# A fused attention and mixture kernel on one core: the rows of the first mixture's output transposed by VectorE in 32x32 blocks and stored in 128-byte runs

## The chip, the cores and the metric

One core of a Trainium2 chip runs the whole program in one launch. The metric is the time of one execution on the device in microseconds. The engines of the core are TensorE (PE in the profile, its weight loads PEld), VectorE (DVE), ScalarE (ACT), GpSimd (POOL) and SyncE (SP), which issues all DMA transfers of this kernel.

## What is computed

Three stages, all in float32, on 2304 tokens of 512 numbers (4 batches of 576 tokens).

```python
# landmark attention, 4 batches x 8 heads x 576 tokens x 64
q_lm, k_lm = means over 18 tokens of q, k          # 32 landmarks
A, Bm, C = sm(q, k_lm), sm(q_lm, k_lm), sm(q_lm, k)
Z = six steps of Z = 2 Z - Z Bm Z                   # inverse of Bm
x = A Z C v                                         # tokens x 512
# first mixture ("moe"): a gated layer over all tokens
xn = x / rms(x) * g
x = (silu(xn @ w_gate) * (xn @ w_val)) @ w_out      # 512 -> 1536 -> 512
# second mixture ("moe2"): a token with x @ w_skip > 0 goes to its best of 8 experts
out = x;  out[t] += prob * relu(x[t] @ w1[e]) @ w2[e]
```

The output of the first mixture is needed twice: with its 512 numbers along the partitions, as the matmuls of the second mixture take it, and as rows of tokens in `out`, to which the second mixture adds.

## The kernel before

The tokens go through the first mixture in 8 units of 288 (half a batch each; `NH` = 288). For a unit, `run_unit` makes 12 blocks of the hidden layer. A block is a gate product `pg` and a value product `pv`, each of 6 matmuls into a tile of 128x288 in PSUM (four such buffers, `acc`); ScalarE takes the tanh of `pg` (`h<-pg`), VectorE does two multiplications (`h<-h,pg`, `h<-h,pv`), ScalarE and GpSimd split the result into a high and a low part (`h_t`). Then `project` makes the unit's output `o` from the 12 blocks, and `evacuate` puts it into `x2T`: 128 partitions x 4 chunks x 288 tokens, so the 512 numbers lie along partitions and chunks. There is one `x2T` buffer.

`finish(u, x2T)`, a generator that is run in pieces beside the next unit's blocks, does the rest: it stores `x2T` into the scratch tensor `xT_d` (L897), makes the logits of the second mixture (`lp`, copied to `lps`, then `lg`), and writes the tokens' rows to `out`. For each of the unit's two tiles of 128 tokens it does four 128x128 transposes on TensorE (`x2t`, L933), a copy from PSUM by VectorE (L937) and a store of 256 KB in runs of 2 KB (L938). For the last 32 tokens VectorE transposes 32x32 blocks (L924), and four stores of 16 KB in runs of 128 bytes put the blocks in place (L929). `lps` and the row buffers `x2` share one buffer. Every second unit then does the routing (`rM`, stored to `m_d`).

Beside the units run the attention of the next batch (loads `kq` and `vt`, products `sk`, `sq`, `cT`) and the products `P` of its result with the weights (loads `wl`, `wr`). In the last unit (7) the second mixture is made ready: `list_pairs` makes the list of pairs of expert and batch that have tokens (`lst`, later `rest`), SP reads it, then come the loads of the first pair's tokens (`x2r`, L1068) and first weights (`w1r`, L1048; four buffers for both), which ScalarE (`xsh<-x2r`, `P<-w1r`), GpSimd and VectorE split into high and low parts. After unit 7, `mixture` runs the first pair: products `ph` into relu, `w2r` loads of the second weights (L1061), the loads `old` of the rows of `out` (L1085), the products `py`, the stores. In this run there are three pairs, the third in a loop.

`slot` decides how far the side generators go, by running sums of estimated work on each engine (`busy`, in which a TensorE transpose counts too). A scheduler then sets the order of the instructions on each engine from the dependencies; each engine and SP's queue run their instructions strictly in that order. All instructions of the four compute engines go through one helper, so that they have one line in the profile (L59); they are told apart by their tiles' names. The profile shortens `x2` to `x`.

Of the kernel before, what the change touches and what calls it, by code (L numbers as in the profile page):

```python
# [6 lines left out]
F32 = mybir.dt.float32  # L7
# [12 lines left out]
KC, FC = DM // 128, DF // 128  # L20
E, DF2 = 8, 1024
FC2 = DF2 // 128
NH = S // 2
NQ = 3
PC = 256
UT = (128, 128, 32)
# [37 lines left out]
def attention_moe_kernel(  # L64
# [4 lines left out]
    V, A, G, PE = (  # L69
        Paced(e, busy, n)  # L70
        for e, n in (
            (nc.vector, "V"), (nc.scalar, "A"), (nc.gpsimd, "G"), (nc.tensor, "P")
        )
    )
    SP = nc.sync
# [10 lines left out]
    def b3(ap, n):  # L86
        return ap.unsqueeze(2).to_broadcast([ap.shape[0], ap.shape[1], n])
# [55 lines left out]
    def bank(name):  # L143
        return pb.tile([128, 512], F32, name=name, tag="b")
# [5 lines left out]
    ident = const.tile([128, 128], F32, name="ident")  # L150
# [583 lines left out]
    def x2_tile(dt):  # L734
        return wk.tile([128, 2, DM], dt, name="x2", tag="x2")
# [157 lines left out]
    def finish(u, x2T):  # L893

        b, half = u // 2, u % 2
        u0 = NH * u
        SP.dma_start(xT_d[:, :, u0 : u0 + NH], x2T)  # L897
        yield

        lp = bank("lp")[:, 0:NH]  # L900
        for c in range(KC):
            PE.matmul(
                lp[32 * c : 32 * c + 32, :], wcat[:, c], x2T[:, c],
                start=True, stop=True,
            )
        lps = x2_tile(F32)[:, 0, 0:NH]
        A.copy(lps, lp)
        yield
        lg = bank("lg")
        for t, m in enumerate(UT):  # L910
            PE.matmul(
                lg[0:m, 32 * t : 32 * t + E + 1], lps[:, 128 * t : 128 * t + m],
                ident4[:, 0 : E + 1], start=True, stop=True,
            )
        lg = lg[:, 0:96].rearrange("p (t e) -> p t e", t=3)[:, :, 0 : E + 1]
        A.copy(lgs[:, 3 * half : 3 * half + 2, :], lg[:, 0:2])
        A.copy(lgs[0:32, 3 * half + 2, :], lg[0:32, 2])
        yield
        for t, m in enumerate(UT):
            ts = slice(128 * t, 128 * t + m)  # L920
            if t == 2:

                x2 = x2_tile(F32)[:, 0, 0:128].rearrange("p (c d) -> p c d", c=KC)
                V.transpose(x2, x2T[:, :, ts])  # L924
                ov = out[u0 + 256 : u0 + NH, :].rearrange(
                    "t (c q d) -> q t c d", c=KC, q=4
                )
                for q in range(4):
                    SP.dma_start(ov[q], x2[32 * q : 32 * q + 32])  # L929
                continue  # L930
            pt = bank("x2t")
            for c in range(KC):
                PE.transpose(pt[0:m, 128 * c : 128 * c + 128], x2T[:, c, ts], ident)  # L933
            if t % 2 == 0:
                x2s = x2_tile(F32)
            x2 = x2s[:, t % 2]
            V.tensor_copy(x2[0:m], pt[0:m])  # L937
            SP.dma_start(out[u0 + 128 * t : u0 + 128 * t + m, :], x2[0:m])  # L938
            yield
        if half == 0:  # L940
            return

        L8 = lgs[:, :, 0:E]
        mx = rt.tile([128, NT], F32, name="rmx")
        V.tensor_reduce(mx, L8, AX.X, ALU.max)
        d = rt.tile([128, NT, E], F32, name="rd")
        V.tensor_tensor(d, L8, b3(mx, E), ALU.subtract)
        ex = rt.tile([128, NT, E], F32, name="rex")
        A.activation(ex, d, AF.Exp)
        V.scalar_tensor_tensor(d, d, 0.0, rank, ALU.is_equal, ALU.mult)  # L950
        V.tensor_reduce(mx, d, AX.X, ALU.max)
        M = rt.tile([128, NT, E], F32, name="rM")
        V.tensor_tensor(M, rank, b3(mx, E), ALU.is_equal)
        yield
        s = rt.tile([128, NT], F32, name="rs")
        V.tensor_reduce(s, ex, AX.X, ALU.add)
        V.tensor_scalar(s, s, 1e-9, None, ALU.add)
        V.reciprocal(s, s)
        V.scalar_tensor_tensor(s, lgs[:, :, E], 0.0, s, ALU.is_gt, ALU.mult)
        V.tensor_tensor(M, M, b3(s, E), ALU.mult)  # L960

        V.tensor_reduce(Ms[:, b], M.rearrange("p t e -> p e t"), AX.X, ALU.add)
        for i in range(2):
            r0 = b * S + NH * i
            SP.dma_start(
                m_d[r0 : r0 + 256, :].rearrange("(t p) e -> p t e", p=128),
                M[:, 3 * i : 3 * i + 2],
            )
            SP.dma_start(m_d[r0 + 256 : r0 + NH, :], M[0:32, 3 * i + 2])
        yield  # L970
# [230 lines left out]
    def run_unit(u, before):  # L1201
# [23 lines left out]
        for c in range(KC):  # L1225
            if u == 0:
                ps = pss[c]
            else:
                ps = accbank("o")[:, 0:NH]
                for f in range(0, FC, 2):  # L1230
                    project(c, ps, (f, f + 1))
                    slot()
            evacuate(x2T, c, ps)
        fin.append(finish(u, x2T))
        side.insert(0, fin[0])

# [178 lines left out]
```

## Time and profile before

| | us |
|---|---|
| median of 3 executions | 700.03 (697.22 to 702.12) |
| the profiled execution | 697.77 |
| its span, first to last instruction | 695.9 |
| TensorE busy in it | 644.3 (93%) |
| VectorE busy | 447.8 (64%) |
| ScalarE busy | 273.8 (39%) |
| GpSimd busy | 144.0 (21%) |
| mean granted TensorE clock | 0.960 of full speed |

Matmuls overlap, so that the busy share of TensorE is not its use at peak; a matmul of 288 columns takes 300 ns from start to end, while the next one starts some 0.13 us behind it. The granted clock is a share of the full 2.4 GHz; 0.5 is the lower level of 1.2 GHz. 1.9 us of the profiled execution lie outside the span.

### The profile page before, as it was taken

The numbers are of one execution on the slowest core, as the hardware profiler recorded it, in microseconds if no ns is written. First come the engines' busy times: TensorE is split into PE (matmuls) and PEld (weight loads), VectorE is DVE, ScalarE is ACT, GpSimd is POOL, SyncE is SP. The second block draws the span as 40 slices with busy tenths as digits, with TensorE's granted clock in tenths as the row PEclk, the third lists the DMA queues.
The fourth block names the chain that finished last, engine by engine and source line by source line (L and its number), as shares of the span: only waits on it lengthen the run. The fifth ranks groups of instructions, "written<-read, shape, count | busy, mean of one in ns | idle before, by whom it ended". The sixth has DMA issues, their size and how long they took to land.

```text
span 695.9 us, 13178 instructions
## 1 busy us (share of the span) xinstructions
PE 644.3 (93%) x4895; PEld 560.5 (81%) x4895; DVE 447.8 (64%) x1004; ACT 273.8 (39%) x613; POOL 144.0 (21%) x162
## 2 busy tenths in 40 slices
PE   4578499999999999999999999999889999999997
PEld 4456167977977988978988968899889988988985
DVE  5874999979778687895768775541623455353451
ACT  0743778433235413433422442331533253243240
POOL 4000026313201301400310211130642024022020
PEclk9755799999999999999999999999999999999999
DMA  8677574652267523176512143400541375454454
GB/s 294 230 253 244 217 247 163 179 157 73 63 154 176 145 82 116 56 174 168 127 47 67 42 108 74 128 5 35 161 124 65 103 225 186 137 155 156 138 157 154
DMA packets 79440, 97.18 MB, mean 140 GB/s; under 512 B 16016, under 2 KB 58000, under 8 KB 79376
## 3 DMA queue, kind: packets, MB, share of 16 engines
q1 hardware_dynamic: 79376, 96.33, 46.0%
q8 instruction: 39, 0.64, 0.4%
q14 instruction: 25, 0.20, 0.1%
HBM read 76.97 MB, written 19.34 MB: 138 GB/s over the span
## 4 chain that ended last, share of the span: by engine, by line
PE 75%; DVE 11%; DMA 4%; ACT 4%; issue 2%; SPq 1%; POOL 1%; DVEq 0%; ACTq 0%; POOLq 0%
PE o L59 18%; PE py L59 11%; PE ph L59 11%; PE pv L59 10%; PE pg L59 9%; PE P L59 3%; PE sq L59 2%; PE sk L59 2%; DVE wo L59 2%; PE nr L59 1%; DMA kq<-in_q_dram 1%; DVE h L59 1%; DVE rbs L59 1%; DVE P L59 1%; DMA wr<-in_moe_w_val_dram 1%
## 5 line engine op out<-in xcount | busy, mean ns | idle before, releaser
L59 PE MATMUL o<-h_t,wo 128*128 128x288 f32 x1152 | 166.1, 300 | 2.6 <-DVE h L59 1.0
L59 PEld LDWEIGHTS o<-h_t,wo 128*128 128x128 f32 x1152 | 156.7, 189 | 10.3 <-issue 5.9
L59 POOL TENSOR_TENSOR h_t<-h,h_t 128x288 fp32r<-128x288 f32 x96 | 81.8, 855 | 354.5 <-ACT h_t L59 347.3
L59 PE MATMUL pg<-ap_t,P 128*128 128x288 f32 x576 | 101.6, 305 | 14.6 <-ACT P L59 8.9
L59 PEld LDWEIGHTS pg<-ap_t,P 128*128 128x128 f32 x576 | 83.5, 191 | 26.4 <-issue 16.5
L59 PE MATMUL pv<-ap_t,P 128*128 128x288 f32 x576 | 101.1, 304 | 0.3 <-DVE h L59 0.2
L59 PEld LDWEIGHTS pv<-ap_t,P 128*128 128x128 f32 x576 | 83.7, 191 | 5.1 <-issue 3.4
L59 PE MATMUL ph<-xsh,P 128*128 128x288 f32 x384 | 78.1, 297 | 0.0
L59 DVE SCALAR_TENSOR_TENSOR h<-h,pg 128x288 f32<-128x288 f32 x96 | 42.7, 447 | 36.8 <-ACT h L59 36.3
L59 PEld LDWEIGHTS ph<-xsh,P 128*128 128x128 f32 x384 | 62.0, 188 | 0.6 <-issue 0.5
L59 ACT ACTIVATE h<-pg 128x288 f32<-128x288 f32 x96 | 39.2, 409 | 48.4 <-PE pg L59 47.1
L59 PE MATMUL ph<-xsl,P 128*128 128x288 f32 x192 | 56.8, 296 | 0.0
L59 ACT CAST h_t<-h 128x288 fp32r<-128x288 f32 x96 | 41.2, 431 | 28.4 <-DVE h L59 28.4
L59 PE MATMUL py<-wo,h_t 128*128 128x512 f32 x210 | 51.6, 396 | 0.0
L59 PEld LDWEIGHTS py<-wo,h_t 128*128 128x128 f32 x210 | 39.6, 188 | 9.7
L59 DVE TENSOR_TENSOR h<-h,pv 128x288 f32<-128x288 f32 x96 | 42.4, 448 | 6.9 <-PE pv L59 3.2
L59 DVE STREAM_TRANSPOSE T<-kq 64x576 f32<-64x576 f32 (+1 forms) x40 | 35.5, 888 | 5.9 <-DMA kq<-in_k_dram 4.4
L59 PEld LDWEIGHTS ph<-xsl,P 128*128 128x128 f32 x192 | 36.2, 189 | 0.1
L59 ACT CAST P<-P 128x512 fp32r<-128x512 f32 x48 | 26.3, 585 | 22.9 <-PE P L59 21.3
L59 POOL TENSOR_TENSOR P<-w1r,P 128x512 fp32r<-128x512 f32 x16 | 20.6, 1289 | 70.1 <-ACT P L59 70.1
L59 DVE TENSOR_TENSOR P<-P,P 128x512 fp32r<-128x512 f32 x48 | 31.6, 678 | 3.7 <-ACT P L59 3.7
L59 DVE SCALAR_TENSOR_TENSOR h_t<-ph,h_t 128x288 fp32r<-128x288 f32 (+2 forms) x45 | 14.6, 352 | 28.1 <-ACT h_t L59 28.1
(223 smaller groups left out, 903.9 us busy)
## 6 DMA issues: line engine op xcount, KB each, us to landing
wl<-wg_d SPq DMA_DIRECT2D x36, 256.0 KB, 4.7
wr<-wv_d SPq DMA_DIRECT2D x32, 256.0 KB, 5.5
w1r<-in_moe_w_dram SPq DMA_DIRECT2D x32, 256.0 KB, 3.4
wr<-in_moe_w_gate_dram SPq DMA_DIRECT2D x6, 1024.0 KB, 7.8
wr<-in_moe_w_val_dram SPq DMA_DIRECT2D x6, 1024.0 KB, 5.8
wo<-in_moe_w_dram SPq DMA_DIRECT2D x24, 256.0 KB, 5.3
kq<-in_k_dram SPq DMA_DIRECT2D x8, 576.0 KB, 4.5
kq<-in_q_dram SPq DMA_DIRECT2D x8, 576.0 KB, 3.9
```

The costliest lines, as they stand in the source:

```text
L59: return f(*args, **kw)
```

## The change

The rows of a unit are no longer made in three tiles. VectorE transposes 32x32 blocks of two chunks at a time over all 288 tokens (128 x 576 numbers to an instruction), twice for a unit. Behind each of the two come 8 stores, one for each chunk and each of its four groups of 32 partitions: 32 partitions x 9 blocks x 32 numbers, so 288 runs of 128 bytes, 36 KB. TensorE's transposes, their PSUM tile and VectorE's copies out of it are gone. The second transpose writes the single `x2` buffer that the first 8 stores read. A unit has 16 stores where there were 6, the program 128 where there were 48.

```diff
@@ finish(u, x2T) @@
-        for t, m in enumerate(UT):
-            ts = slice(128 * t, 128 * t + m)
-            if t == 2:
-                x2 = x2_tile(F32)[:, 0, 0:128].rearrange("p (c d) -> p c d", c=KC)
-                V.transpose(x2, x2T[:, :, ts])
-                ov = out[u0 + 256 : u0 + NH, :].rearrange(
-                    "t (c q d) -> q t c d", c=KC, q=4
-                )
+        ov = out[u0 : u0 + NH, :].rearrange(
+            "(a t) (c q d) -> q c t a d", t=32, c=KC, q=4
+        )
+        for c in range(0, KC, 2):
+            x2 = x2_tile(F32).rearrange("p c n -> p (c n)")[:, 0 : 2 * NH].rearrange(
+                "p (c n) -> p c n", n=NH
+            )
+            V.transpose(
+                x2.rearrange("p c n -> p (c n)"),
+                x2T[:, c : c + 2].rearrange("p c n -> p (c n)"),
+            )
+            for i in range(2):
                 for q in range(4):
-                    SP.dma_start(ov[q], x2[32 * q : 32 * q + 32])
-                continue
-            pt = bank("x2t")
-            for c in range(KC):
-                PE.transpose(pt[0:m, 128 * c : 128 * c + 128], x2T[:, c, ts], ident)
-            if t % 2 == 0:
-                x2s = x2_tile(F32)
-            x2 = x2s[:, t % 2]
-            V.tensor_copy(x2[0:m], pt[0:m])
-            SP.dma_start(out[u0 + 128 * t : u0 + 128 * t + m, :], x2[0:m])
+                    SP.dma_start(
+                        ov[q, c + i],
+                        x2[32 * q : 32 * q + 32, i].rearrange(
+                            "t (a d) -> t a d", d=32
+                        ),
+                    )
             yield
```

The scheduler's orders differ in many places, since other instructions stand between the same neighbours. Three places matter below. The lines behind L938 have moved up by one.

The first is ScalarE in unit 7, from the fourth block of the hidden layer on (`h<-pg` is the tanh of a block, `xsh<-x2r` splits a load of the first pair's tokens). Before:

```order
L59 ACTIVATE h<-pg 128x288
L59 CAST xsh<-x2r 128x576 x2
L59 CAST h_t<-h 128x288
L59 CAST xsh<-x2r 128x576
L59 ACTIVATE h<-pg 128x288
L59 CAST xsh<-x2r 128x576
L59 ACTIVATE h<-pg 128x288
```

Now, from the third block on:

```order
L59 ACTIVATE h<-pg 128x288 x2
L59 CAST h_t<-h 128x288 x2
L59 ACTIVATE h<-pg 128x288 x2
L59 CAST xsh<-x2r 128x576
L59 CAST h_t<-h 128x288
L59 CAST xsh<-x2r 128x576
L59 CAST h_t<-h 128x288
L59 CAST xsh<-x2r 128x576
L59 ACTIVATE h<-pg 128x288
L59 CAST xsh<-x2r 128x576
```

The first split stood behind four tanh of the unit and stands behind six now.

The second is ScalarE at the end of the same unit, where it splits the last four weight loads of the first pair (`P_666<-w1r`). Before:

```order
L59 CAST P_666<-w1r 128x512 x2
L59 ACTIVATE h<-pg 128x288
L59 CAST P_666<-w1r 128x512
L59 ACTIVATE h<-pg 128x288
L59 CAST P_666<-w1r 128x512
L59 CAST h_t<-h 128x288 x2
L59 ACTIVATE h<-pg 128x288
```

Now:

```order
L59 CAST P_662<-w1r 128x512 x2
L59 ACTIVATE h<-pg 128x288
L59 CAST h_t<-h 128x288
L59 CAST P_666<-w1r 128x512 x2
L59 ACTIVATE x2T<-o 128x288
L59 CAST P_666<-w1r 128x512 x2
```

The four splits stood between the unit's last three tanh and stand behind the last one now.

The third is SP's queue in the first pair of the second mixture, ahead of the last two loads of second weights (`w2r`, which begin behind the last row of the first fence and of the second fence's loads `old`). Before:

```order
L929 DMA out_dram<-x_6322 128x1x32 x4
L1085 ISA
L1085 DMA old_6480<-out_dram 128x512
L1085 ISA
L1085 DMA old_6482<-out_dram 128x512
L1085 ISA
L1085 DMA old_6484<-out_dram 128x512
L1085 ISA
L1085 DMA old_6486<-out_dram 64x512
L1061 ISA
L1061 DMA w2r<-in_moe_w_dram 128x512
```

Now:

```order
L968 DMA m_d<-rM 32x8
L1017 TENSOR_LOAD rest
L1017 ISA x2
L932 DMA out_dram<-x_6310 32x9x32 x8
L1075 ISA
L1075 DMA mc<-m_d 128x4x1
L1078 ISA
L1078 DMA mc<-m_d 64x1
L1084 ISA
L1084 DMA old_6470<-out_dram 128x512
```

A read of the list `rest` and the unit's last 8 stores now stand ahead of the loads `mc`, all five `old` and the two `w2r`.

## Rows read from the trace of the kernel before

**Rows 1.** The page: busy time by engine, and the chain by engine.

```profile
PE 644.3 (93%) x4895; PEld 560.5 (81%) x4895; DVE 447.8 (64%) x1004; ACT 273.8 (39%) x613; POOL 144.0 (21%) x162
...
PE 75%; DVE 11%; DMA 4%; ACT 4%; issue 2%; SPq 1%; POOL 1%; DVEq 0%; ACTq 0%; POOLq 0%
```

**Rows 2.** Windows of 50 us: length, busy by engine, PEclk, DMA share, GB/s.

```profile
50.00:100.00 50.00, 37.10 (x182) 23.41 (x182) 38.02 (x57) 31.00 (x54) 2.89 (x4) 0.73 0.66 230
...
250.00:300.00 50.00, 49.97 (x448) 44.03 (x442) 43.26 (x112) 16.30 (x49) 11.05 (x13) 1.00 0.26 84
...
600.00:650.00 50.00, 50.00 (x293) 44.86 (x293) 21.71 (x41) 17.84 (x35) 10.74 (x8) 1.00 0.43 135
```

**Rows 3.** TensorE in order of time: start us, us; two groups of transposes, what follows.

```profile
488.10 1.04 PE L59 MATMUL x2t<-ident,x2T 128*128 128x128 f32 x8
488.89 0.65 PE L59 MATMUL pg<-ap_t,P 128*128 128x288 f32 x3
...
543.58 0.60 PE L59 MATMUL x2t<-ident,x2T 128*128 128x128 f32 x4
...
543.94 0.38 PE L59 MATMUL ph<-xsh,P 128*128 128x288 f32 x1
...
544.16 0.29 PE L59 MATMUL ph<-xsl,P 128*128 128x288 f32 x1
```

**Rows 4.** VectorE's groups with shapes kept apart, and the small transpose by its tile.

```profile
L59 DVE COPY x<-x2t 128x512 f32<-128x512 f32 x16 | 10.6, 683 | 1.9 <-ACT h L59 1.4 <-PE x2t L59 0.4
...
L59 DVE STREAM_TRANSPOSE AT<-sT 128x576 f32<-128x576 f32 x8 | 6.2, 773 | 1.1 <-POOL sT L59 1.1
...
L59 DVE STREAM_TRANSPOSE x<-x2T x8: 293/304/311, 209.1 to 548.9; 128x128 f32<-128x128 f32 x8
```

**Rows 5.** SP's issues by line: ns min/median/max; under the first its landing.

```profile
L929 SPq DMA_DIRECT2D out_dram<-x x32: 590/600/662, 209.4 to 551.2; - x32
...
DMA to landing us min/median/max: 1.8/1.9/3.4
...
L938 SPq DMA_DIRECT2D out_dram<-x x16: 338/362/952, 163.5 to 546.0; - x16
...
L897 SPq DMA_DIRECT2D xT_d<-x2T x8: 582/594/604, 141.5 to 532.7; - x8
```

**Rows 6.** Window in which the four L929 stores of one unit are issued.

```profile
209.40:212.10 2.70, 2.70 (x23) 2.70 (x22) 2.70 (x7) 0.48 (x2) 0.00 (x0) 1.00 0.09 15
```

**Rows 7.** TensorE in unit 7, in order of time: blocks and two gaps.

```profile
490.18 0.96 PE L59 MATMUL pg<-ap_t,P 128*128 128x288 f32 x6
...
491.77 0.95 PE L59 MATMUL pg<-ap_t,P 128*128 128x288 f32 x6
...
497.31 1.81 PE L59 MATMUL pg<-ap_t,P 128*128 128x288 f32 x6 [2.22 <-DVE h L59]
...
509.69 1.07 PE L59 MATMUL pg<-ap_t,P 128*128 128x288 f32 x6 [2.70 <-DVE h L59]
```

**Rows 8.** ScalarE in unit 7, in order of time.

```profile
492.06 1.37 ACT L59 CAST xsh<-x2r 128x576 fp32r<-128x576 f32 x2 [0.19 <-DMA x2r<-xT_d]
...
495.79 0.67 ACT L59 CAST xsh<-x2r 128x576 fp32r<-128x576 f32 x1 [2.03 <-DMA x2r<-xT_d]
496.36 0.40 ACT L59 ACTIVATE h<-pg 128x288 f32<-128x288 f32 x1
...
507.73 0.62 ACT L59 CAST P<-w1r 128x512 fp32r<-128x512 f32 x1 [0.75 <-DMA w1r<-in_moe_w_dram]
508.25 0.40 ACT L59 ACTIVATE h<-pg 128x288 f32<-128x288 f32 x1
```

**Rows 9.** Windows of 5 us in unit 7; PEclk is the eighth number.

```profile
495.00:500.00 5.00, 2.78 (x12) 2.69 (x12) 2.56 (x6) 3.07 (x7) 2.72 (x3) 0.72 0.75 245
500.00:505.00 5.00, 5.00 (x38) 5.00 (x37) 3.57 (x8) 3.06 (x8) 4.54 (x4) 0.94 0.43 106
...
510.00:515.00 5.00, 5.00 (x28) 5.00 (x27) 2.24 (x5) 1.94 (x5) 3.10 (x4) 0.66 0.64 204
```

**Rows 10.** SP's issues in order of time: unit 7, then the first pair.

```profile
489.23 2.01 SPq L1068 DMA_DIRECT2D x2r<-xT_d  x4
...
554.90 0.94 SPq L1061 DMA_DIRECT2D w2r<-in_moe_w_dram  x2
```

**Rows 11.** The first pair: ScalarE's split of that load, TensorE's first use.

```profile
558.97 0.62 ACT L59 CAST wo<-w2r 128x512 fp32r<-128x512 f32 x1 [1.75 <-DMA w2r<-in_moe_w_dram]
...
561.39 1.56 PE L59 MATMUL py<-wo,P 128*128 128x512 f32 x6
```

## The prediction

> **What bounds the kernel now.** I read the page first: TensorE is busy 93% of the span, and the chain that ends last is 75% TensorE and 11% VectorE [rows 1]. The windows of 50 us say where: up to about 100 us it waits for others and gets a lower clock (0.73 in the second window), but from 250 to 300 us and from 600 to 650 us it has no idle time [rows 2]. The transposes that go lie between 153 and 544 us, all in that part. There, time taken off TensorE's queue comes off the run, unless the new work makes TensorE wait. So the next views were TensorE in order of time, for what a transpose costs and for gaps, then ScalarE and SP around the gaps.
>
> **TensorE's transposes.** 64 of them go, in 12 places: 8 groups of four and 4 of eight. A group of eight holds the queue from 488.10 to 488.89 us, 0.79 us, a group of four from 543.58 to 543.94, 0.36 us [rows 3]. 4 x 0.79 + 8 x 0.36 = 6.0 us. The first matmul behind such a group takes 0.38 us where its neighbour takes 0.29 [rows 3]; twelve times 0.09 are 1.1 us more, part of which another switch of shape would cost anyway. Other groups last somewhat longer than the two shown. Bounds 6.0 to 7.4, taken: **-6.8 us**.
>
> **VectorE.** Out: 16 copies of 0.683 and 8 small transposes of 0.304 us, together 13.4 us. In: 16 transposes of 128 x 576; the same operation and shape from SBUF to SBUF takes 0.773 us [rows 4], together 12.4 us. VectorE has slack in the stretches where TensorE is full, so -1.0 us of busy time is worth nothing: **0**. Per 128x128 block TensorE is the cheaper engine, 0.36 / 4 = 0.09 us of its queue against 0.773 / 4.5 = 0.17 us [rows 3, 4]. The Trainium skill ("VectorE: DVE Perf Modes", Rules for kernel authors) says to use TensorE for a 128x128 transpose where the result may go to PSUM, which speaks against this change. By its rule the work would be left where it is, and the sum would be 0; the rows agree with it on the price of a block alone, but TensorE's result has to be copied out by VectorE, and TensorE is the full engine.
>
> **SP's queue.** Out for a unit: 2 stores of 0.362 and 4 of 0.600 us, 3.1 us. In: 16 stores of 288 runs. No row shows that shape. The nearest is L929, also 32 partitions in runs of 128 bytes, 0.600 us with 128 runs; the store of `x2T` has 512 runs and takes 0.594 us [rows 5], so the time does not grow with the runs. I take 0.60, bounds 0.36 (as L938) and 1.35 (0.60 x 288 / 128, if it did grow). At 0.60 a unit's stores take 9.6 us, 6.5 us more than before, 52 us in the program. SP mostly waits for others, so only what stands behind the stores matters (below). Moving the bytes is cheap: while the four L929 stores go out, the 16 DMA engines are busy 0.09 of 2.7 us, 3.9 engine-us, at 15 GB/s, 40 KB or 316 runs [rows 6]: 12.3 ns a run. A unit's 4608 runs are 3.5 us of all engines, spread over 9.6 us of issue. The Trainium skill ("DMA: Bandwidth & Descriptors", Issuing engines are not separate DMA queues) calls the time to start a DMA usually small beside the DMA itself. Here a row says otherwise, 0.60 us to issue against 18 runs x 12.3 ns = 0.22 us on each engine; by the page the delays priced next would be near 0 and the time 1.8 us lower.
>
> **The added wait.** The second transpose of a unit waits on VectorE until the first 8 stores have landed: 8 x 0.60 + 1.9 = 6.7 us [rows 5] behind the first. Behind it in VectorE's queue stand the multiplications of the blocks, for which TensorE's PSUM buffers wait. In the new order the fewest blocks between the two are about five (units 1 and 3), at 1.59 us each, from 490.18 to 491.77 [rows 7], 8.0 us; in units 5 and 7 they make up 9.6 us, in the others some 20 to 40 instructions stand between. So the wait is covered, by 1.2 us at the least: **0**. The cover is gone from 0.76 us an issue on.
>
> **Unit 7.** Here TensorE stands still twice for multiplications on VectorE, 2.22 and 2.70 us [rows 7]. VectorE waits for the tanh on ScalarE, and that stands behind splits of loads: 2.03 us for `x2r`, then the tanh at 496.36; later `w1r`, then the tanh at 508.25 [rows 8]. After each gap the clock falls to the lower level for a while: mean 0.72, 0.94 and 0.66 in three windows of 5 us [rows 9], 1.4 + 0.3 + 1.7 = 3.4 us. Both together cost 8.3 us. In the new order the first split stands two tanh later, 3.2 us, and the last four `w1r` splits stand behind the last tanh. Against that, `x2r` itself comes later: the list's instructions on VectorE stand behind the 0.773 us transpose and a further block's multiplications, so I put the loads of 489.23 [rows 10] at some 490.5 to 491. The third load then lands about 1.2 to 1.7 us later than before, at 497, while its tanh would be due at some 495.5; TensorE has two blocks of PSUM in hand and stands still for about 0.8 us. The second gap goes, since what its splits wait for is no longer ahead of a tanh. Left are 0.8 us and perhaps one fall of the clock, 1.7: gain 5.8 to 7.5. Bounds +2 (the loads later still) and -8.3; since the landing is guessed, I take **-5.0 us**.
>
> **First pair.** The last two `w2r` now come behind the list `rest`, 8 stores and all of `old`. `rest` is read near 550 in the old clock, then 8 x 0.60, two `mc` and five `old` at some 0.5 us each: 560.8 in place of 554.90 [rows 10]. The old load was split 4.1 us after its issue [rows 11]; now that is 564.9, and 1.9 us more for the two parts give 566.8. TensorE begins `py` at 561.39 [rows 11] and in the new order does 30 matmuls that need no part of them first, 6.4 us at 0.21 us, and all this 0.8 us earlier: needed at about 567. Bounds 0 to +3, taken **+0.7**. Loads of `kq`, `vt`, `wl` and `wr` that stand behind stores in the other units come 2 to 6 us later; most are fetched long ahead: 0 to +3, taken **+1.1**.
>
> **Sum:** -6.8 - 5.0 + 0.7 + 1.1 = -10.0 us on the profiled 697.77. That execution is 2.3 us under the median; I take the same off the median of 700.03: **690.0 us**.
>
> **Rivals.**
> *Unit 7 keeps its gaps.* Loads later by as much as the splits have been moved leave both gaps: -6.8 + 1.8 = -5.0, 695.0. For it: ScalarE's order follows the scheduler's idea of when loads land, and the trace shows it 2.03 us too early before. Against it: the second gap's splits have left their place altogether.
> *More goes.* All 8.3 us of unit 7 and the delays at 0: -15.1, 684.9.
> *The loads come much later in unit 7*, the gaps grow by 3 us and the clock falls once more: -6.8 + 1.8 + 4.7, 699.7.
> *SP becomes the bound (slower).* If issue grows with the runs, 1.35 us, the wait of the second transpose is 8 x 1.35 + 1.9 = 12.7 us. In units 1 and 3 VectorE stops for 4.7 us, in 5 and 7 for 3.1; less 1.6 us of matmuls in hand that is 3.1, 3.1, 1.5 and 1.5 us of TensorE, and four falls of the clock at 1.7: 16.0 us. `w2r` comes 8 x 0.75 = 6 us later still and TensorE waits for it: +6.7 in place of 0.7. 16.0 + 6.7 - 6.8 = +15.9, 715.9. It decides from 0.76 us an issue on. Against it: 0.594 us for 512 runs [rows 5].
>
> **How the numbers follow.** Forecast 0.45; gaps kept 0.30; more 0.13; loads much later 0.06; SP the bound 0.06. About 1% (7 us) is what a measurement of this kernel can tell from no change, so faster by over 1% is below 693.0. That holds for nearly all of the forecast, for more, and for a fifth of the first rival, whose price is uncertain by some 3 us: 0.41 + 0.13 + 0.06 = 0.60. Slower by over 1% is the last rival alone, 0.06; within 1% the rest, 0.34. The range of 684.5 to 697.5 takes in the forecast, the first rival and most of "more".
>
> **What would show it.** No `x2t` on TensorE; issue of the new stores at 0.60 us; VectorE's idle time ahead of the second transposes under 1 us in all; the two gaps at `pg` in unit 7 under 2 us together, and a clock near 1.00 there; `py` of the first pair starting on `w2r` in time. I am wrong if the new stores take over 0.76 us to issue, if ScalarE still waits for `x2r` ahead of a tanh, or if the new orders open gaps where there were none.

## The result and the profile after

The new kernel takes 688.74 us (median of 4 runs, 686.14 to 691.38) against 699.82 for the old one beside it: a ratio of 0.985, 95% interval 0.982 to 0.9881. A second series gave 0.9898, 0.9874 to 0.9923. So it is about 7 to 11 us faster; 690.0 had been forecast.

The page of the new kernel, engines and chain, answers to [rows 1]:

```profile
PE 638.6 (93%) x4831; PEld 552.4 (80%) x4831; DVE 452.9 (66%) x996; ACT 275.1 (40%) x613; POOL 146.0 (21%) x162
...
PE 66%; DVE 14%; DMA 6%; issue 5%; ACT 5%; POOL 2%; SPq 2%; DVEq 0%; ACTq 0%; POOLq 0%
```

TensorE has 64 instructions and 5.7 us less. The 5.7 us are not the price of the transposes: ahead of the first store of `x2T` TensorE is busy 2.7 us longer in this trace than before, and in stretch 6 (below) 3.5 us less, most of which is clock. To see where the time went, I cut the run where SP stores `x2T` of a unit (L897): stretch n runs from the store of unit n to that of unit n + 1. Stretch 6 holds the blocks of unit 7, stretch 2 those of unit 3 with the finish of unit 2. The table is worked out from the start times of these stores and the end of TensorE's last instruction, in us:

| kernel | first store at | six stretches 0 to 5 | stretch 6 | last store to end | first store to end |
|---|---|---|---|---|---|
| before | 141.5 | 340.8 | 50.4 | 158.5 | 549.7 |
| after | 143.3 | 337.8 | 43.1 | 158.6 | 539.4 |
| after, second trace | 145.9 | 337.7 | 43.0 | 157.6 | 538.3 |

The first store comes later in the new kernel's traces, though both kernels' instructions stand in the same order up to there; more on that at the end. From the first store on, the new kernel is 10.3 to 11.4 us shorter: 3.0 in six stretches, 7.3 in stretch 6, little or nothing behind it.

These windows of before (new rows: stretches 1, 2 and 6) show length, busy time by engine, PEclk, DMA share, GB/s:

```profile
215.50:266.20 50.70, 50.34 (x483) 44.26 (x484) 37.39 (x96) 17.05 (x47) 10.84 (x13) 1.00 0.54 139
266.20:325.20 59.00, 58.74 (x551) 51.62 (x550) 48.40 (x116) 22.23 (x59) 10.70 (x13) 1.00 0.47 123
482.40:532.70 50.30, 45.38 (x324) 43.78 (x323) 21.01 (x43) 19.54 (x45) 21.27 (x20) 0.93 0.37 112
```

The same three of after:

```profile
216.70:265.50 48.80, 48.38 (x442) 43.48 (x441) 36.02 (x86) 17.21 (x44) 10.79 (x13) 1.00 0.47 112
265.50:327.10 61.60, 59.97 (x555) 51.13 (x554) 51.47 (x126) 23.64 (x61) 10.99 (x13) 1.00 0.49 124
481.00:524.10 43.10, 41.86 (x316) 40.02 (x315) 23.00 (x42) 19.27 (x46) 21.95 (x20) 1.00 0.48 131
```

Stretch 6 lost 3.7 us of idle time (4.92 to 1.24) and its clock rose from 0.93 to 1.00 (the falls of [rows 9] are gone). Stretch 2 got *longer*, by 2.6 us: its TensorE stands idle for 1.63 us in place of 0.26 and does 1.2 us more, since work moved across the stores: beside its eight transposes, stretch 1 has 33 instructions fewer (442 for 483), stretch 0 has 23 more and stretch 2 has 12 more (555 for 551). Over stretches 0 to 5, by the same windows, TensorE's work falls from 334.8 to 330.7 us (48 transposes, 0.085 each) and its idle time rises from 6.0 to 7.1.

What is left of the two gaps of [rows 7], TensorE in order of time:

```profile
496.32 1.07 PE L59 MATMUL pg<-ap_t,P 128*128 128x288 f32 x6 [0.29 <-DVE h L59]
...
499.12 1.07 PE L59 MATMUL pg<-ap_t,P 128*128 128x288 f32 x6 [0.93 <-DVE h L59]
```

And ScalarE there, answering to [rows 8]: the split of `x2r` waits 0.41 us in place of 2.03, and the `w1r` wait of 3.56 us stands behind the last tanh:

```profile
494.80 0.67 ACT L59 CAST xsh<-x2r 128x576 fp32r<-128x576 f32 x1 [0.41 <-DMA x2r<-xT_d]
...
510.90 0.62 ACT L59 CAST P<-w1r 128x512 fp32r<-128x512 f32 x1 [3.56 <-DMA w1r<-in_moe_w_dram]
```

The new stores by their line (ns min/median/max, and landing in us), beside [rows 5], then VectorE's new group with the idle time ahead of it:

```profile
L932 SPq DMA_DIRECT2D out_dram<-x x128: 315/453/1893, 165.3 to 545.9; - x128
...
DMA to landing us min/median/max: 1.5/1.7/4.6
```

```profile
L59 DVE STREAM_TRANSPOSE x<-x2T 128x576 f32<-128x576 f32 x16 | 12.4, 776 | 5.3 <-PE lg L59 3.5 <-DMA xT_d<-x2T 1.3 <-issue 0.3
```

A store costs SP 0.453 us, less than the 0.600 of the small stores before. No idle time of VectorE ahead of these transposes ends on a store to `out`, so the added wait costs nothing. The idle time on `lg` and `xT_d` stands ahead of the first transpose of a unit; ahead of the second ones there are 0.3 us in all, and the second starts 9.9 us behind the first at the least.

### The profile page after: what moved, and what is told of

It reads as the page before. It is cut to its first block, busy times and chain, and to the rows that moved or that the text cites. A ratio compares the mean times of both kernels' runs of the same rounds, so it can differ in the third digit from the quotient of the medians.

```text
span 687.3 us, 13145 instructions
## 1 busy us (share of the span) xinstructions
PE 638.6 (93%) x4831; PEld 552.4 (80%) x4831; DVE 452.9 (66%) x996; ACT 275.1 (40%) x613; POOL 146.0 (21%) x162
## 4 chain that ended last, share of the span: by engine, by line
PE 66%; DVE 14%; DMA 6%; issue 5%; ACT 5%; POOL 2%; SPq 2%; DVEq 0%; ACTq 0%; POOLq 0%
PE o L59 17%; PE pv L59 10%; PE pg L59 9%; PE ph L59 9%; PE py L59 8%; PE P L59 3%; PE sq L59 2%; DVE wo L59 2%; PE nr L59 2%; PE sk L59 2%; DVE h L59 1%; ACT wo L59 1%; DMA x2r<-xT_d 1%; DVE s L59 1%; DVE T L59 1%
## 5 line engine op out<-in xcount | busy, mean ns | idle before, releaser
L59 POOL TENSOR_TENSOR h_t<-h,h_t 128x288 fp32r<-128x288 f32 x96 | 83.7, 877 | 350.5 <-ACT h_t L59 327.9
L59 PE MATMUL pv<-ap_t,P 128*128 128x288 f32 x576 | 98.6, 301 | 1.6 <-DVE h L59 1.3
```

The costliest lines, as they stand in the source:

```text
L59: return f(*args, **kw)
```

## The experiments

None of these kernels leaves out work; 2, 5 and the second of 6 add some that has no use.

**1. The new way in some of the units.** `if u < 6:` (or `if u >= 6:`) ahead of the new lines, the old lines in the `else`.

> The new way in units 0 to 5 (six of eight), the old one in units 6 and 7. ScalarE's order in unit 7 is then the old one, with both splits of x2r ahead of the fifth tanh. Theory A: six units' transposes, 6/8 of 6.8, about 5 us under before, 695; the two gaps of 2.2 and 2.7 us in unit 7 are there as before. Theory B: 0 to 3 us under before, 697 to 700, with gaps elsewhere that the old kernel has not.

Measured: ratio 0.9954 (0.9922 to 0.9986), 3.2 us under before. Unit 7 keeps its gaps:

```profile
498.24 1.70 PE L59 MATMUL pg<-ap_t,P 128*128 128x288 f32 x6 [1.87 <-DVE h L59]
...
510.25 1.07 PE L59 MATMUL pg<-ap_t,P 128*128 128x288 f32 x6 [2.28 <-DVE h L59]
```

> The new way in units 6 and 7 alone (the second half of the last mixture's pair of units), the old one in units 0 to 5. ScalarE's order in unit 7 is the new one. Theory A: 1.7 us of transposes and 5 to 8 us of gaps and clock in unit 7, so 7 to 9 us under before, 691 to 693. Theory B: nearly the whole gain of the new kernel, 9 to 11 us under before, 689 to 691. If unit 7's order is worth little, 2 us under before, 698.

Measured: ratio 0.9918 (0.9888 to 0.9948), 5.7 us under before; gaps of 0.63 and 0.59, stretch 6 in 43.0 us. Together the two parts give 8.9 us, all of the change 7 to 11. The parts add up, as in theory A, with each some 2 us smaller than it said; the 3.2 us of the first part lie between the two theories, so that it is the 5.7 us and the gaps that speak for A. Stretch 6 of the first kernel takes 48.2 us where before took 50.4, though its instructions stand in the same order there on every engine: timing alone moves unit 7 by some 2 us. A piece of theory B is there too: with the new way in units 0 to 5, stretch 2 has 1.6 us of idle time that before has not.

**2. Dead transposes.** The new kernel with TensorE's transposes back, and no reader:

```diff
+            pt = bank("x2t")
+            for k in range(KC):
+                PE.transpose(
+                    pt[:, 128 * k : 128 * k + 128], x2T[:, k, 64 * c : 64 * c + 128], ident
+                )
```

> The new kernel with the 64 transposes put back on TensorE, eight a unit, written to a PSUM bank that nobody reads; the stores stay as in the new kernel, so this only adds work without use. Theory A (the transposes' time in TensorE's queue is most of the gain, about 6.8 of it, and unit 7's new order the rest): about 6 to 7 us over the new kernel's 688.7, so 695; unit 7's gaps stay small (under 2 us together) and the clock there at 1.00. Theory B (the gain is unit 7's order and its clock; elsewhere what is taken off TensorE comes back as new gaps): within 2 us of the new kernel, 689 to 691.

Measured: ratio 0.9903 (0.9867 to 0.9939), median 693.19. Beside the new kernel's 0.985 that is 3.7 us more, beside its second 0.9898 nearly nothing, so the times alone don't settle it. From first store to end it takes 544.4 us, 5.0 and 6.1 over the two traces of after, which speaks for theory A; experiment 5 sets it right beside its base. Stretch 6 shows that unit 7's gain does not need the transposes gone:

```profile
487.30:531.30 44.00, 42.41 (x324) 40.82 (x323) 21.90 (x42) 19.46 (x45) 22.03 (x20) 1.00 0.47 127
```

**3. The preparation later, in the old kernel.** `f in (3, 6, 11)` for `f in (1, 4, 8)`.

> The kernel before with all its transposes, but with the three steps of the next mixture's preparation taken up later in unit 7 (behind blocks 3, 6 and 11 instead of 1, 4 and 8), so that ScalarE's splits of the x2r and w1r loads stand behind later tanh. If the gaps and the clock in unit 7 come from the place of these splits, whatever the transposes: 5 to 8 us under before, 692 to 695, gaps under 2 us together and a clock of 1.00. If the gain in unit 7 needs the transposes or VectorE's copies gone: about 700, the gaps still there.

Measured: ratio 0.9982 (0.9951 to 1.0014): no difference that can be told from the times (3.4 us at the most). The step moves the loads along with their splits, and so the edit did not do what it was meant to. SP issues `x2r` at 496.43 in place of 489.23 [rows 10], and the split waits for it ahead of a tanh as before. ScalarE, then TensorE, in order of time:

```profile
500.34 1.33 ACT L59 CAST xsh<-x2r 128x576 fp32r<-128x576 f32 x2 [1.93 <-DMA x2r<-xT_d]
```

```profile
503.54 1.41 PE L59 MATMUL pg<-ap_t,P 128*128 128x288 f32 x6 [1.92 <-DVE h L59]
```

The split stands behind eight tanh here and behind four before, and a tanh still stands behind it. In this one trace stretch 6 takes 47.3 us, 3.1 less than before, with 2.9 us of gaps in place of 4.9: the second gap has become 1.0 us.

**4. The list and the loads of `x2r` earlier**, in both kernels:

```diff
-            if u == 2 * B - 1 and f in (1, 4, 8):
+            if (u == 2 * B - 2 and f == 11) or (u == 2 * B - 1 and f in (4, 8)):
                 next(pre)
```

> The kernel before with the first of the next mixture's three preparation steps (the list of pairs and the x2r loads) taken up behind block 11 of unit 6 instead of block 1 of unit 7, the other two behind blocks 4 and 8 as before. All transposes stay on TensorE. The x2r loads then go out before the stores of unit 6 and their splits stand ahead of unit 7's tanh. Theory A (the gaps and the clock's fall in unit 7 come from splits that wait for loads ahead of a tanh): gaps under 1.5 us together if w1r lands in time, clock 1.00, unit 7 shorter by 4 to 6.6 us, the run 4 to 6 us under before, 693 to 695. Rival (the gaps come from the copies and transposes of the old way on VectorE and TensorE): the gaps stay above 3.5 us together, the run within 1.5 us of before.

Measured: ratio 0.9928 (0.9905 to 0.995), 5.0 us under before, with all transposes on TensorE. SP issues `x2r` at 464.50. Stretch 6:

```profile
482.90:526.40 43.50, 41.27 (x312) 40.06 (x311) 18.89 (x35) 16.91 (x41) 18.64 (x18) 1.00 0.24 78
```

It is 6.9 us shorter than before (1.5 of that moved to stretch 5, which is 44.6 for 43.1), the clock is 1.00 throughout, and 2.2 us of gaps are left, somewhat more than expected; 1.25 of them follow a split of `w1r` that waits 1.60 us ahead of a tanh. The rival, that the gaps came from the old copies and transposes, falls: they are all still there. ScalarE's splits of `x2r` wait even longer than before:

```profile
467.43 1.34 ACT L59 CAST xsh<-x2r 128x576 fp32r<-128x576 f32 x2 [3.24 <-DMA x2r<-xT_d]
```

But they stand behind the last tanh of unit 6 (461.76) and ahead of the first of unit 7, and TensorE has no gap in stretch 5. The way from load to split is no longer than before, 2.9 us (464.50 to 467.43) for 2.8 (489.23 to 492.06). What counts is whether TensorE waits for a tanh that stands behind the waiting split.

> The same move of the list in the new kernel. Theory A: the 1.2 us of gaps that are left in unit 7 go, nothing else: 0 to 1.5 us under the new kernel, 687 to 689, and 5 to 6 us under the run above, which is the transposes' queue time alone. Rival (unit 7's gain belongs to the stores and transposes): unit 7 as in the new kernel, 689, and no less than 9 us under the run above.

Measured: ratio 0.987 (0.984 to 0.99), 2.0 us under the new kernel beside it (0.9898, below) and 4.0 under the run above. Once more:

> The new kernel with the list taken up early, once more, as the base of the three kernels beside it: 0.987 of before, unit 7 in 41.5 us.

Measured: 0.9841 (0.9815 to 0.9866). From first store to end the two traces show 538.3 and 538.8, against 539.4 and 538.3 for the new kernel: level. So it beats the old kernel surely and the new one by 2 us at most, within the intervals. Stretch 6 has 0.8 us of idle time left:

```profile
480.70:522.10 41.40, 40.63 (x304) 39.19 (x303) 19.83 (x34) 16.92 (x41) 19.01 (x18) 1.00 0.31 82
```

The new kernel beside the first of these:

> The new kernel once more, beside the three below: 0.985 of before by all theories. Its trace serves as a second look at unit 7 (gaps of 1.2 us together, clock 1.00) and at the stores' 0.45 us.

Measured: 0.9898; gaps of 0.27 and 0.94 in unit 7, clock 1.00, stores 0.453 us.

**5. The transposes' price without unit 7.** The early list, with the dead transposes of experiment 2.

> The base with the 64 transposes back on TensorE without a reader. Unit 7's waits are out of the way here, so this prices the transposes' queue time by itself. If what TensorE's queue loses comes off the run: 64 x 0.09 = 5.7 us over the base, 694. If part of it only takes the place of gaps that VectorE's new order leaves from unit 1 to 6 (1.0 us in the traces so far): 4 to 5 us over it, 692.5. If the gain was order alone: 0.

Measured: ratio 0.9913 (0.988 to 0.9947) against the base's 0.9841: 5.0 us by the ratios, 6.5 by the medians, 4.3 to 4.9 from first store to end. In stretches 0 to 5 TensorE works 336.8 us for 332.4, and idles 5.6 for 6.9. The windows from first store to end, of this kernel and of the base:

```profile
144.97:688.13 543.16, 536.31 (x4291) 476.95 (x4290) 336.25 (x759) 196.74 (x468) 116.13 (x118) 1.00 0.44 119
141.41:680.24 538.83, 530.89 (x4227) 470.00 (x4226) 337.29 (x759) 195.83 (x468) 116.69 (x118) 1.00 0.44 120
```

64 instructions are 5.4 us of TensorE's work here (6.0 with the other trace of the base, and 6.1 to 6.5 in the pairs of experiment 2), 0.085 to 0.10 us each. So of 5.4 to 6.0 us of queue time some 4.3 to 5 come off the run, the middle case. Its stretch 2 shows where the rest goes:

```profile
269.60:329.30 59.70, 59.70 (x552) 51.77 (x551) 48.74 (x117) 23.38 (x59) 10.73 (x13) 1.00 0.49 121
```

No idle time here, where the base has 1.63: the dead transposes partly fill gaps.

**6. Why stretch 2 has gaps.** The base with `if u != 2:` ahead of the new lines and the old ones in the `else`:

> The base with the old way in unit 2 alone. In the new kernel the stretch from unit 2's store of x2T to unit 3's takes 61.6 us where it took 59.0 before, with TensorE idle 1.6 us in place of 0.26; that is where the missing part of the transposes' gain goes. If the two long transposes on a VectorE that is busy 84% there are its cause: the stretch falls to 59 to 60 us, TensorE's gaps there to under 0.5 us, and the run stands level with the base or up to 1.5 us under it. If the cause is the order in units 0 and 1 (work shifted across the store): the stretch stays at 61 to 62, and the run is 0.7 us over the base.

Measured: ratio 0.9857 (0.9829 to 0.9885), 1.1 us over the base by the ratios, within the intervals. The stretch does not come back to 59:

```profile
264.80:327.80 63.00, 61.20 (x563) 52.09 (x562) 51.94 (x127) 23.29 (x61) 10.74 (x13) 1.00 0.46 121
```

1.80 us of idle time remain with the old way in that very unit. That is nearer to the other expectation, an order that was changed in units 0 and 1. Then each of VectorE's transposes twice:

> The base with each of VectorE's 16 long transposes made twice, with the same result: 16 x 0.78 = 12.4 us more on VectorE, no more on TensorE. If VectorE has room wherever TensorE is full, as the prediction took it: 0 to 1 us over the base. If it is short of room around unit 2 and in the units with attention beside them: 2 to 4 us over, with new gaps of TensorE between 145 and 310 us that end on VectorE.

Measured: ratio 0.9817 (0.9792 to 0.9842): no slower than the base. VectorE's group and stretch 2:

```profile
L59 DVE STREAM_TRANSPOSE x<-x2T 128x576 f32<-128x576 f32 x32 | 24.7, 771 | 5.0 <-PE lg L59 3.5 <-DMA xT_d<-x2T 1.3
```

```profile
268.90:329.70 60.80, 60.35 (x555) 51.54 (x554) 52.33 (x125) 23.31 (x61) 10.76 (x13) 1.00 0.45 109
```

12.3 us more on VectorE, and TensorE idles 0.45 us in this stretch in place of 1.63. My theory that the long transposes crowd VectorE there falls twice: they can stay out and the gaps stay, and they can double and the gaps go. What is left is the order in which small steps of the attention and the multiplications of the blocks stand on VectorE, which differs in each of these kernels: the new kernel's gaps there are four, of 0.36 to 0.51 us, each on a result of VectorE (`bdq`, `h`, `Y`, `sq`). That is argued, not shown: which rows make the gaps was not isolated.

**7. Twice as many stores.** Each store cut in two, of runs of 64 bytes (`"(a t) (c q w d) -> q w c t a d"` with w = 2).

> The new kernel with each store cut into two, of runs of 64 bytes: 32 stores a unit in place of 16, the same bytes in twice the packets. If a store costs SP 0.45 us whatever its bytes, a unit's stores take 14.4 us in place of 7.2, and the second transpose waits until 16 x 0.45 + 1.7 = 8.9 us behind the first, against 8.0 us of blocks in units 1 and 3: VectorE waits about 1 us there, and the last two w2r of the first pair come 3.6 us later, when the room was about 3: 1 to 4 us over the new kernel, 690 to 693. Rival (SP is far from binding, everything behind the stores has room): 689. If the DMA engines bind (packets of 64 bytes), landing goes from 1.7 to over 2.5 us and the run over 695.

Measured: ratio 0.9969 (0.9944 to 0.9994), median 695.47, 4.3 us over the new kernel beside it (5.0 by the ratios), a little past the 1 to 4 expected. Issue and landing of the halved stores:

```profile
L933 SPq DMA_DIRECT2D out_dram<-x x256: 315/453/2067, 165.9 to 557.6; - x128
...
DMA to landing us min/median/max: 1.5/1.7/4.6
```

Both are as for whole ones, so the DMA engines are not what binds. A second transpose now has to wait for 16 stores, 16 x 0.453 + 1.7 = 8.9 us, and still no idle time of VectorE ahead of its 16 transposes ends on them: the second starts 10.8 us behind the first at the least. SP in unit 7 and the first pair, and TensorE's gaps there:

```profile
493.47 2.05 SPq L1068 DMA_DIRECT2D x2r<-xT_d  x4
...
563.65 0.96 SPq L1061 DMA_DIRECT2D w2r<-in_moe_w_dram  x2
```

```profile
502.37 1.29 PE L59 MATMUL pg<-ap_t,P 128*128 128x288 f32 x6 [2.13 <-DVE h L59]
...
568.66 0.73 PE L59 MATMUL py<-wo,h_t 128*128 128x512 f32 x2 [1.42 <-ACT wo L59]
570.02 2.14 PE L59 MATMUL py<-wo,h_t 128*128 128x512 f32 x8 [0.64 <-POOL wo L59]
```

The first pair shows what more stores do: its last `w2r` go out 33.5 us behind unit 7's store of `x2T` in place of 27.1, and TensorE waits 2.06 us for them. From the last store to the end the kernel is 1.8 us longer than the first trace of the new one.

The rest of its loss is not shown to be SP's. Unit 7's gap is back, with a fall of the clock (0.97 in the 50 us around it), but `x2r` goes out 8.3 us behind the store of `x2T`, hardly later than the 8.0 of the new kernel; the scheduler has put the first split one tanh earlier, and the last one ahead of the tanh that it stood behind. Stretches 3 and 4 together are 3.7 us longer (stretch 4 alone 66.6 us for 61.4, with 12 instructions more), and none of TensorE's gaps in stretch 4 ends on a load.

## Why the prediction was right, point by point

**TensorE's transposes** were taken at -6.8, bounds 6.0 to 7.4. Measured: 5.4 us of work where they went (64 x 0.085), 5.4 to 6.5 where they were put back, and 4.3 to 6.1 of the run in experiments 2 and 5. The mechanism holds; the term was too large by up to 1.4 us, for the most part the 1.1 us for a slower first matmul behind a group. The 6.0 us from starts of instructions [rows 3] fit; the modelled durations beside them added what did not come off.

**VectorE at 0** holds: even 12.3 us more of it cost nothing measurable. On the Trainium skill ("VectorE: DVE Perf Modes", Rules for kernel authors), which sends a 128x128 transpose to TensorE: per block TensorE stays cheaper (0.085 to 0.10 against 0.776 / 4.5 = 0.17 us), and the run is still faster by the work moved, since TensorE was full and VectorE was not.

**SP at 0.60 a store** was too high: 0.453 for 288 runs of 128 bytes, the same for 288 runs of 64. The added wait is then 8 x 0.453 + 1.7 = 5.3 us against the 8.0 of cover that was forecast, 9.9 in the trace. On the Trainium skill ("DMA: Bandwidth & Descriptors", Issuing engines are not separate DMA queues), by which issue is usually small beside the transfer: here 0.453 us of issue stand against an estimated 18 x 12.3 ns = 0.22 on each engine. The same bytes in twice the stores put off the first pair's `w2r` by 6.4 us in experiment 7.

**Unit 7 at -5.0**: stretch 6 fell by 7.3 us, 0.7 of it eight transposes, so 6.6 against bounds of +2 and -8.3. The forecast of 0.8 us of gap and perhaps one fall of the clock met 1.24 us and no fall. That this gain is the order of splits and loads, and not the transposes, is shown by experiment 4: most of it is there in the old kernel too once list, loads and splits are moved ahead. The 6.6 rests on a single trace of before; against the 48.2 us that the same order takes in experiment 1 the gain is 4.4. So the cautious -5.0 for "guessed landing" was too small by 1.6 at the most, and the traces don't tell that from what timing alone does to unit 7.

**First pair at +0.7**: 0. SP issued the last `w2r` at 551.22, 27.1 us behind unit 7's store of `x2T`; before it was 22.2, and the forecast of 560.8, in the times of the old trace, is 28.1. So the delay was a microsecond less than forecast. ScalarE split it at 556.25, and the low parts were done at 558.3 and 558.8. TensorE began `py` at 551.90, and its 30 matmuls that need none of this lasted until 558.91, 0.23 us each and not 0.21, so there was no gap, by a small margin:

```profile
551.22 0.96 SPq L1060 DMA_DIRECT2D w2r<-in_moe_w_dram  x2
```

**Other loads at +1.1**: one gap of TensorE from the first store on ends on a load, `wl`, and it did before (0.70 us, now 0.86 and 1.07). Behind the last store the first trace has a gap of 0.76 us, behind VectorE's wait for `mc` of the second pair; the second trace has none. In their place came what the prediction named as a way to be wrong, new gaps from a new order: idle time is up by 1.1 us over stretches 0 to 5 (1.4 more in stretch 2, 0.3 less elsewhere). The size fits the +1.1, the cause does not.

**The sum** over the traces: 4.1 of work in stretches 0 to 5, less 1.1 of idle time, and 7.3 in stretch 6: -10.3 from first store to end, the forecast -10.0. That the total is so near is in part luck: errors cancel, 1.4 too much for the transposes against 1.6 too little for unit 7. The prediction has no term for the start of the program, where the new trace is 1.7 us behind; the two profiled executions differ by 8.8 us.

**The rivals.** *Unit 7 keeps its gaps* is what experiment 1 shows with units 6 and 7 left in the old way: median 696.2, near the 695.0 given. *SP becomes the bound* had the right resource and the wrong place: at double the issue time a unit, past its point of 0.76, the second transposes still do not wait, since they stand 10.8 us apart and not 8.0; it is `w2r` behind the stores that TensorE waits for.

## What to carry to other kernels

Where one engine is full, a dearer operation on an engine with room can be a gain, and its price is what it takes from the full engine's queue, by starts in order of time. A change that issues more instructions on a queue is paid by whatever stands behind them there; list those loads and their first use before costing the wait that the change itself adds. A split or cast that waits for a load on an in-order engine belongs behind that engine's critical work: moving the list, the loads and the splits there was worth 5.0 us in the old kernel, about half of the change itself.

## What the runs showed beside this

The issue time of a store did not depend on its bytes: 0.453 us for 36 KB in runs of 128 bytes and for 18 KB in runs of 64, 0.600 for L929's 128 runs [rows 5]. Why the smaller store is dearer stays open.

The start differs between executions of one kernel. Two traces of the new kernel have the first store of `x2T` at 143.3 and 145.9 us, and the granted clock of the first 20 us at 0.91 and 0.84:

```profile
0.00:20.00 20.00, 11.06 (x48) 9.86 (x48) 10.82 (x41) 1.85 (x4) 8.34 (x26) 0.91 0.90 286
```

```profile
0.00:20.00 20.00, 11.89 (x48) 10.60 (x48) 9.97 (x36) 1.70 (x3) 8.31 (x26) 0.84 0.90 282
```

The four traces in which units 0 to 5 are as before have it at 140.5 to 142.8, the ten others at 141.4 to 145.9; the means are 141.5 and 144.1. The granted clock of the first 20 us is 1.00 in all four and in one of the ten, 0.83 to 0.91 in the other nine. That makes chance unlikely: some 2 us of the gain from the first store on are lost ahead of it. Why is open; no run was made to tell.
